# An earlier TensorE warm-up, x's first rows loaded in column halves, and two more single w1 loads in a squared-ReLU MLP

## The chip, the cores and the metric

The kernel runs on one core of one Trainium2 chip. The metric is device time in microseconds (us), median over the runs of a kernel. One run differs from the next by up to about 1.5 us, so every comparison is made between runs on the same chip, and ratios come with a 95% interval. "In the head" means the first 10 us of the kernel.

## The reference

```python
# B, S, D, F = 1, 2048, 576, 4608; all bf16
def reference(x, w1, b1, w2, b2):
    h = jnp.einsum("bsd,df->bsf", x, w1) + b1
    r = jnp.where(h > 0, h, 0)
    return jnp.einsum("bsf,fd->bsd", r * r, w2) + b2
```

## The kernel before

x has four blocks of 512 rows; a block has four row tiles of 128. D = 576 is four chunks of 128 columns and a rest of 64. The kernel keeps w1 in SBUF as pairs of 64-row halves (`w1h`) and runs 36 by 9 by 4 such half-height products at full width, then the second product. All of that is dense. The part that matters here is the head: before the steady matmuls can start, the first 512 rows of x have to be loaded and transposed on TensorE, and the first four column tiles of h are computed from a plainly loaded piece of w1 (`qn`, chunks 0 to 3 of 128 by 512, "quads") so that the big w1 load has time to arrive.

```python
load_x(nc.sync, 0)          # 144 KB each: 128 rows of x, all 576 columns
load_x(nc.scalar, 1)
load_quad(nc.sync, 0)       # 128 KB each: w1 rows c*128.., columns 0..511
load_quad(nc.scalar, 1)
load_quad(nc.sync, 2)
load_x(nc.scalar, 2)
load_x(nc.sync, 3)
load_quad(nc.scalar, 3)
nc.scalar.activation(out=warm[:], ..., func=ACT.Relu)   # brings the activation table
for h in range(2):
    load_rest(nc.sync, h)                               # w1's last 64 rows, 64 KB in all
for j0, n in ((2, 1), (3, 1), (4, 1), (5, 1), (6, 2), (8, 2), (10, 2), (12, 2), (14, 4)):
    for h in range(2):
        load_w1(nc.sync, h, j0, n, slice(0, NH))        # pairs of w1, n at a time
# issue_at_barrier: loads that wait for nothing are moved ahead of the opening barrier's wait
...
for i in range(NWARM):      # 5 warm-up matmuls, 128x512, on constants
    nc.tensor.matmul(wps[:], lhsT=ones[:, 0:P], rhs=ones[:], ...)
...
transpose_chunks(0, (0,), (V,))        # half 0 = row tiles 0 and 1; chunk 0, copied out by VectorE
transpose_chunks(0, (1,), (A,))
fill(HALF)                             # one more matmul on constants, 128x256
full_mm(0, 0)                          # half 0, chunk 0: four matmuls 128x256
transpose_chunks(0, (2, NC), (A, V))
full_mm(0, 1)
transpose_chunks(0, (3,), (A,))
full_mm(0, 2)
transpose_chunks(1, (0, 1), (V, A))    # needs row tiles 2 and 3
full_mm(0, 3)                          # needs w1 chunk 3
transpose_chunks(1, (2, NC), (A, V))
full_mm(1, 0)
...                                    # half 1, the rest, then the steady a_step(0, 2), a_step(0, 3) ...
```

## Time and profile before

| | before |
|---|---|
| median of the first three runs | 290.34 us (289.94 to 290.49) |
| span in the profile | 289.1 us |
| TensorE busy | 285.0 us (99%) |
| first warm-up, first transpose, first real matmul | 0.78, 2.87, 3.67 us |
| first steady matmul (w1h) | 9.90 us |
| release of TensorE's full clock, by the clock record | 6.29 us |

The clock record is the trace's own list of the stretches in which TensorE's clock was granted in full; "release" is the start of the first one. In the views, PE is TensorE's matmuls, PEld its weight loads, DVE VectorE, ACT ScalarE, POOL GpSimd and SP SyncE; a q behind the name marks what the engine's instruction queue issues, such as a load.

From the page of before, the busy times and the chain of work that ended last:

```profile
span 289.1 us, 4821 instructions
...
PE 285.0 (99%) x2068; PEld 187.6 (65%) x2079; DVE 79.3 (27%) x195; ACT 95.5 (33%) x153; POOL 1.5 (1%) x8
...
PE 99%; issue 0%; DVE 0%
```

So TensorE is the bound, and only its head can be shortened. The timeline of TensorE in before (start us, length us, line, operation, count) shows the head. Two things are to be seen. Nothing idles by more than 0.16 us. And the clock is half at first: the four matmuls of 3.67 us start 0.21 us apart, those of 6.79 us 0.11 us apart. The page's granted-clock row reads full speed throughout; this half clock is seen only in the spacing of the matmuls and in the clock record.

```profile
0.78 2.29 PE L150 MATMUL wps<-const-bfloat16-1.0 128*128 128x512 bf16 x5 [0.78 <-PEq L340]
2.87 0.63 PE L167 MATMUL tp<-ident,w_sb 128*128 128x128 bf16 x4
3.30 0.42 PE L153 MATMUL wps<-const-bfloat16-1.0 128*128 128x256 bf16 x1
3.67 1.01 PE L213 MATMUL ph<-w_sb 128*128 128x256 bf16 x4
...
5.97 0.76 PE L213 MATMUL ph<-w_sb 128*128 128x256 bf16 x4
6.57 0.39 PE L167 MATMUL tp<-ident,w_sb 128*128 128x128 bf16 x4
6.79 0.60 PE L213 MATMUL ph<-w_sb 128*128 128x256 bf16 x4
...
9.90 1.46 PE L198 MATMUL ph<-w_sb,w1h 64*128 64x512 bf16 x12
```

The weight loads of before show one wait for w1 later, at pair 6 (in brackets: idle time before the group, and what ended it):

```profile
17.76 1.30 PEld L198 LDWEIGHTS <-w1h 64*128 64x128 bf16 x14 [0.21 <-DMA w1h<-in_w_dram]
```

### The profile page before, as it was taken

The numbers are of one execution on the slowest core, as the hardware profiler recorded it, in microseconds if no ns is written. First come the engines' busy times: TensorE is split into PE (matmuls) and PEld (weight loads), VectorE is DVE, ScalarE is ACT, GpSimd is POOL, SyncE is SP. The second block draws the span as 40 slices with busy tenths as digits, with TensorE's granted clock in tenths as the row PEclk, the third lists the DMA queues.
The fourth block names the chain that finished last, engine by engine and source line by source line (L and its number), as shares of the span: only waits on it lengthen the run. The fifth ranks groups of instructions, "written<-read, shape, count | busy, mean of one in ns | idle before, by whom it ended". The sixth has DMA issues, their size and how long they took to land.

```text
span 289.1 us, 4821 instructions
## 1 busy us (share of the span) xinstructions
PE 285.0 (99%) x2068; PEld 187.6 (65%) x2079; DVE 79.3 (27%) x195; ACT 95.5 (33%) x153; POOL 1.5 (1%) x8
## 2 busy tenths in 40 slices
PE   8999999999999999999999999999999999999996
PEld 5568888888888888888855444444444444444454
DVE  1644454444445444444420011111100111111111
ACT  3666666666666666666620000000000000000000
POOL 2000000000000000000000000000000000000000
PEclk9999999999999999999999999999999999999999
DMA  7999998900300006100000100000000000000000
GB/s 206 217 216 197 178 198 178 328 14 2 114 11 0 3 2 196 51 0 2 0 2 19 20 20 20 20 23 0 20 20 23 20 20 20 23 22 20 20 23 20
DMA packets 34229, 18.01 MB, mean 62 GB/s; under 512 B 19348, under 2 KB 34208, under 8 KB 34208
## 3 DMA queue, kind: packets, MB, share of 16 engines
q1 hardware_dynamic: 33600, 17.14, 25.0%
q10 hardware_dynamic: 576, 0.56, 0.6%
q8 instruction: 16, 0.26, 0.4%
q14 instruction: 5, 0.04, 0.0%
q0 software_dynamic: 32, 0.01, 0.0%
HBM read 11.94 MB, written 2.36 MB: 49 GB/s over the span
## 4 chain that ended last, share of the span: by engine, by line
PE 99%; issue 0%; DVE 0%
PE ph L198 47%; PE po L316 43%; PE pc L302 5%; PE ph L213 2%; PE wps L150 1%; PE tp L167 1%; PE ph L239 0%; DVE o_sb L318 0%; PE wps L153 0%; PE b1T_ps L232 0%
## 5 line engine op out<-in xcount | busy, mean ns | idle before, releaser
L198 PEld LDWEIGHTS <-w1h 64*128 64x128 bf16 x1260 | 115.0, 94 | 21.1 <-DMA w1h<-in_w_dram 0.2
L182 ACT ACTIVATE r<-ph,b1T 128x512 bf16<-128x512 f32 x144 | 90.8, 684 | 48.5 <-PE ph L198 46.6
L198 PE MATMUL ph<-w_sb,w1h 64*128 64x512 bf16 x936 | 101.3, 376 | 0.0
L316 PE MATMUL po<-w_sb,hT 128*128 128x512 bf16 x423 | 92.9, 379 | 0.5
L316 PEld LDWEIGHTS <-hT 128*128 128x128 bf16 x432 | 42.2, 98 | 51.1 <-issue 0.4
L184 DVE TENSOR_TENSOR hT<-r 128x512 bf16<-128x512 bf16 x108 | 45.9, 425 | 54.7 <-ACT r L182 54.7
L318 DVE TENSOR_TENSOR o_sb<-po,b_bc 128x512 bf16<-128x512 f32 (+2 forms) x17 | 11.2, 660 | 116.7 <-PE po L316 109.7
L198 PE MATMUL ph<-xT,w1h 64*128 64x512 bf16 x324 | 35.2, 376 | 0.0
L316 PE MATMUL po<-w_sb,w1h 128*128 128x512 bf16 (+2 forms) x178 | 31.2, 336 | 0.1
L316 PEld LDWEIGHTS <-w1h 128*128 128x128 bf16 x180 | 16.2, 98 | 15.3
L184 DVE TENSOR_TENSOR w1h<-r 128x512 bf16<-128x512 bf16 x36 | 15.3, 425 | 19.7 <-ACT r L182 19.7
L302 PE MATMUL pc<-hT,w_sb 128*64 128x512 bf16 x108 | 15.7, 379 | 0.0
L302 PEld LDWEIGHTS <-w_sb 128*64 128x64 bf16 x144 | 8.1, 110 | 7.6 <-issue 0.4
L302 PE MATMUL pc<-w1h,w_sb 128*64 128x512 bf16 x36 | 7.9, 379 | 0.0
L304 ACT ACTIVATE oc<-pc,b2T 128x512 bf16<-128x512 f32 x2 | 1.4, 687 | 13.8 <-PE pc L302 13.8
L213 PE MATMUL ph<-w_sb 128*128 128x256 bf16 x32 | 5.5, 314 | 0.0
L312 DVE COPY o_sb<-oc 128x64 bf16<-128x64 bf16 x16 | 2.7, 172 | 9.4 <-DMA oc<-oc 9.4
L213 PEld LDWEIGHTS <-w_sb 128*128 128x128 bf16 x32 | 3.3, 112 | 0.7 <-DMA w_sb<-in_w_dram 0.2
L160 DVE COPY w_sb<-tp 128x256 bf16<-128x256 bf16 x5 | 1.5, 291 | 6.5 <-PE tp L167 6.5
L150 PE MATMUL wps<-const-bfloat16-1.0 128*128 128x512 bf16 x5 | 2.3, 622 | 0.8 <-PEq L340 0.8
L167 PE MATMUL tp<-ident,w_sb 128*128 128x128 bf16 x20 | 2.7, 265 | 0.0
L167 PEld LDWEIGHTS <-w_sb 128*128 128x128 bf16 x20 | 2.1, 122 | 0.9 <-DMA w_sb<-in_x_dram 0.6
(28 smaller groups left out, 11.3 us busy)
## 6 DMA issues: line engine op xcount, KB each, us to landing
w_sb<-in_w_dram SPq DMA_DIRECT2D x6, 864.0 KB, 7.4
w1h<-in_w_dram SPq DMA_DIRECT2D x10, 288.0 KB, 7.8
out_dram<-o_sb SPq DMA_DIRECT2D x15, 144.0 KB, 1.7
w1h<-in_w_dram SPq DMA_DIRECT2D x8, 144.0 KB, 3.6
w1h<-in_w_dram SPq DMA_DIRECT2D x2, 576.0 KB, 9.5
w_sb<-in_x_dram SPq DMA_DIRECT2D x2, 144.0 KB, 3.0
w_sb<-in_x_dram ACTq DMA_DIRECT2D x2, 144.0 KB, 3.1
w_sb<-in_w_dram SPq DMA_DIRECT2D x2, 128.0 KB, 3.3
```

The source lines that it names most:

```text
L150: nc.tensor.matmul(wps[:], lhsT=ones[:, 0:P], rhs=ones[:], start=(i == 0), stop=(i == NWARM - 1))
L160: nc.vector.tensor_copy(out=dst, in_=src)
L167: nc.tensor.transpose(tp[:, i * P:(i + 1) * P], xs[:, 2 * half + i, d0:d0 + P], ident[:])
L182: nc.scalar.activation(out=r[:], in_=bk[:], func=ACT.Relu, bias=b1T[:, ft:ft + 1], scale=1.0)
L184: nc.vector.tensor_tensor(out=hT_of(b, ft), in0=r3, in1=r3, op=ALU.mult)
L198: nc.tensor.matmul(bk[h][:], lhsT=w1h[rows, c, j * P:(j + 1) * P], rhs=xT[b][rows, place(h, c), :], start=(i == 0), stop=(i == NH - 1))
L213: nc.tensor.matmul(bk0[q][:, cols], lhsT=qn[:, c, q * P:(q + 1) * P], rhs=xT[0][:, c, cols], start=(half == 0 and c == 0), stop=False, ski ...
L302: nc.tensor.matmul(pc[h * H:(h + 1) * H, :], lhsT=w2(ft, DM, D), rhs=hT_of(2 * pr + h, ft), start=(ft == 0), stop=(ft == NFT - 1))
L304: nc.scalar.activation(out=oc[:, pr, :], in_=pc[:], func=ACT.Identity, bias=b2T[:], scale=1.0)
L312: nc.vector.tensor_copy(out=o_sb[:, DM:D], in_=o_tr[pr][:, jj, h * H:(h + 1) * H])
L316: nc.tensor.matmul(po[:, 0:e - a], lhsT=hT_of(b, ft)[:, jj, :], rhs=w2(ft, a, e), start=(ft == 0), stop=(ft == NFT - 1))
L318: nc.vector.tensor_tensor(out=o_sb[:, a:e], in0=po[:, 0:e - a], in1=b2_bc[:, a:e], op=ALU.add)
```

## The change

The intent: begin the warm-up 0.4 us sooner by placing it ahead of the opening barrier's wait (with its own constant, written by VectorE), bring the first transposes' data sooner by loading only 256 columns of row tiles 0 and 1 first and the other 320 behind w1's chunks 0 and 1, and avoid the wait at pair 6 by loading pairs 6 and 7 singly. The order of the head's work follows the new arrival order. Ten loads in place of eight do not all fit ahead of the barrier: each of the first eight has a completion semaphore of its own, later ones wait for an earlier one to be done. So row tile 3 and chunk 3 are now issued after the barrier.

```diff
-    load_x(nc.sync, 0)
-    load_x(nc.scalar, 1)
+    first, later = slice(0, 2 * P), slice(2 * P, D)
+    load_x(nc.sync, 0, first)
+    load_x(nc.scalar, 1, first)
     load_quad(nc.sync, 0)
     load_quad(nc.scalar, 1)
+    load_x(nc.sync, 0, later)
+    load_x(nc.scalar, 1, later)
     load_quad(nc.sync, 2)
     load_x(nc.scalar, 2)
     load_x(nc.sync, 3)
+    nc.scalar.activation(out=warm[:], ..., func=ACT.Relu)
     load_quad(nc.scalar, 3)
-    nc.scalar.activation(out=warm[:], ..., func=ACT.Relu)
...
-    for j0, n in ((2, 1), (3, 1), (4, 1), (5, 1), (6, 2), (8, 2), ...):
+    for j0, n in ((2, 1), (3, 1), (4, 1), (5, 1), (6, 1), (7, 1), (8, 2), ...):
...
+    one = const.tile([P, 1], BF16, name="one")
+    nc.vector.memset(one[:], 1.0)
+    def warm_at_barrier(nc):   # moves this memset and the 5 warm-up matmuls
+        ...                    # ahead of each engine's wait at the opening barrier
+    nc.at_finalize(warm_at_barrier)
...
-    ones = nc.const_aps.tensor(1.0, [P, SB], BF16)
+    ones = one[:].to_broadcast([P, SB])
...
     transpose_chunks(0, (1,), (A,))
-    fill(HALF)
     full_mm(0, 0)
-    transpose_chunks(0, (2, NC), (A, V))
     full_mm(0, 1)
-    transpose_chunks(0, (3,), (A,))
+    transpose_chunks(0, (2,), (V,))
+    transpose_chunks(0, (3, NC), (A, V))
     full_mm(0, 2)
```

Left out here: w2's chunks 4 and 5, and 2 and 3, each become one load, and b2's last 64 values are loaded by GpSimd. All that happens after 8 us, far ahead of its use.

## The prediction

> **What bounds it.** The page gives a 289.1 us span, TensorE busy 285.0 (99%); the chain of waits is 99% PE. Only the head can be shortened: the timeline has the first w1h matmul (L198) at 9.90 us, and from there PE shows no idle to 60 us (groups view, 0.0 before L198).
>
> In the head (PE timeline): first warm-up 0.78 us, five at 0.427 us apiece; first transpose 2.87; one filler; first real matmul 3.67. 256-column matmuls start 0.213 us apart until about 6.3, then 0.109: the clock doubles 5.5 us after PE's first matmul. The Trainium skill ("TensorE: Matmul & The Clock Gate", Part 1) says the clock is released after a busy, free-running window of about 3.4 us, so the moment varies from run to run. This trace shows the doubling; the variation no trace here shows yet. By that estimate release falls 3.4 to 6.8 us after the start, and one microsecond of it is worth 0.5 us.
>
> **What changes, costed.**
> 1. The warm-up moves ahead of the barrier's wait. PE arrives at the barrier at 0.32 us and is let go at 0.68; its weight load could follow at about 0.39, after VectorE's one-column memset. Gain in start 0.39 us. With an unmoved clock release this is worth half, 0.2 us; if release moves too, 0.39.
> 2. The filler (0.21 us) goes, but it filled a wait for the chunk-0 copy (transpose to copy to matmul, 0.37 us in all): worth 0.
> 3. x's first halves carry 128 KB in place of 288 KB ahead of w1's chunks 0 and 1, which landed at 3.45 and 3.93. At about 270 KB/us (landings between 2.6 and 5.6 us) they land 0.5 us earlier; needed, since PE asks 0.4 us earlier.
> 4. w1's chunk 3 is issued by ScalarE after its table load (1.28 us, ending 3.43) and a wait for an earlier landing: about 3.5 us, not 1.58, so it lands near 6.2 (was 5.56). PE wants it about then. ScalarE's copy of chunk 1 stands behind that issue: about 4.0, not 3.55. Cost 0 to 0.4 us.
> 5. w1 pairs 6 and 7 singly: before, pair 6 landed at 17.72 and PE's weight load had to wait for it (17.76, 0.2 us), so an earlier head would have been lost there. Single halves landed every 0.75 us, so pair 6 now lands near 14.5 and pair 7 near 15.7. Pair 8 (before 20.31, wanted 21.6) slips to about 20.8 and becomes the next floor, some 0.5 us below the old one.
> 6. Merged w2 loads and b2's tail on GpSimd: off the chain (loads at 47 us and later; w2 is wanted after 169): 0.
>
> Bytes and matmuls after 10 us are unchanged, hence 279 us as before. Expected: L198 starts at about 9.4, span about 288.6, a gain of 0.4 to 0.5 us.
>
> **Prediction.** 289.9 us, 8 in 10 between 289.2 and 290.5. Faster by over 2%: 0.01; within 2%: 0.98; slower by over 2%: 0.01.
>
> **What would show it.** Right: first warm-up at 0.35 to 0.45 us; first transpose near 2.5; first real matmul near 3.3; L198 near 9.4; no weight load waiting for w1h at pair 6. Wrong: the warm-up still at 0.7 or later; PE waiting before chunk 1 (ScalarE's copy) or chunk 3 (its landing) for more than 0.4 us; a wait for w1h at pair 8.
>
> **What would make it wrong.** The release of the clock is the widest term: a window more or less is up to 1.7 us either way, larger than the change. New pauses early in the head could make a window count as idle and put release 3.4 us later. Chunk 3 landing late, or pair 8 after 21 us, would give the gain back.

## The result, and the profile after

The changed kernel took 290.74 us (median of 6 runs, 290.55 to 291.05) against 290.41 us (6 runs, 289.94 to 291.31). A ratio here and below is the mean of one kernel's fast runs over the mean of the other's of the same rounds, so not quite the ratio of the medians: 1.0009, interval 0.9992 to 1.0026. On another chip, later, the changed kernel again: 290.88 against 290.29, ratio 1.0019 (1.0000 to 1.0038). Within 2% as predicted, but no gain, and outside the predicted range of 289.2 to 290.5.

The page of after:

```profile
span 288.8 us, 4821 instructions
...
PE 284.7 (99%) x2067; PEld 133.6 (46%) x2078; DVE 79.7 (28%) x197; ACT 95.3 (33%) x152; POOL 3.2 (1%) x11
```

TensorE's timeline in after:

```profile
0.38 2.31 PE L172 MATMUL wps<-one 128*128 128x512 bf16 x5 [0.38 <-DVE one L147]
2.49 0.63 PE L185 MATMUL tp<-ident,w_sb 128*128 128x128 bf16 x4
3.29 1.87 PE L231 MATMUL ph<-w_sb 128*128 128x256 bf16 x8 [0.17 <-DVE w_sb L178]
4.95 0.66 PE L185 MATMUL tp<-ident,w_sb 128*128 128x128 bf16 x6
5.75 0.60 PE L231 MATMUL ph<-w_sb 128*128 128x256 bf16 x4
6.18 0.39 PE L185 MATMUL tp<-ident,w_sb 128*128 128x128 bf16 x4
6.59 0.61 PE L231 MATMUL ph<-w_sb 128*128 128x256 bf16 x4
...
9.71 1.46 PE L216 MATMUL ph<-w_sb,w1h 64*128 64x512 bf16 x12
```

The start came as intended: the warm-up at 0.38, the transposes at 2.49, the first real matmul at 3.29 in place of 3.67. The clock record has the release at 5.26 us, which is 1.03 us before that of the other trace, by itself worth about 0.5 us (half of it, as matmuls run twice as fast afterwards). Still the steady part begins only 0.19 us sooner (9.71 against 9.90). From the first real matmul on, the head took 6.42 us where it had taken 6.23 with a later clock.

The start-to-start times have three new pauses: 0.38 us before 3.29, 0.31 before 5.75 and 0.19 before 6.59. The first two end with a copy of a transposed chunk (chunk 0 and chunk 2), though w1's chunks 0 and 2 landed only 0.1 us before these two ended (3.20 and 5.65). The third is plain in the weight loads of after, which name the loads waited for:

```profile
3.24 1.43 PEld L231 LDWEIGHTS <-w_sb 128*128 128x128 bf16 x8 [0.39 <-DMA w_sb<-in_w_dram]
...
5.69 0.37 PEld L231 LDWEIGHTS <-w_sb 128*128 128x128 bf16 x4 [0.27 <-DMA w_sb<-in_w_dram]
...
6.59 0.33 PEld L231 LDWEIGHTS <-w_sb 128*128 128x128 bf16 x4 [0.19 <-DMA w_sb<-in_w_dram]
```

By the completion records in the two traces (the moment when the last of a load's 16 parts had landed):

| load | before, us | after, us |
|---|---|---|
| x row tiles 0, 1 (after: first 256 columns) | 2.21, 2.62 | 2.04, 2.22 |
| w1 chunks 0, 1 | 3.45, 3.93 | 3.20, 3.63 |
| x's other 320 columns, tiles 0, 1 | with the above | 4.12, 4.32 |
| w1 chunk 2 | 4.70 | 5.65 |
| x row tiles 2, 3 | 4.88, 5.30 | 5.87, 6.11 |
| w1 chunk 3 | 5.56 | 6.54 |

The first four loads came 0.2 to 0.4 us sooner. The last four came about 1 us later, though no byte was added. Chunk 3's first matmul starts 0.05 us after chunk 3 has landed, and the steady part 3.12 us after that. Pair 6 of w1 was complete at 16.38 us in place of 17.72, 1.1 us before its use (9.71 plus four steps of 1.94 us), and no weight load waited for w1h. Chunk 3's load was issued at 3.22 us, while ScalarE's table load was still running:

```profile
2.15 1.28 ACT L118 ACT_TABLE_LOAD   x1 [2.15 <-ACTq L357]
3.22 0.34 ACTq L95 DMA_DIRECT2D w_sb<-in_w_dram  x1
3.45 0.20 ACT L118 ACTIVATE warm<-const-float32-1.0 128x1 f32<-128x1 f32 x1
3.60 0.37 ACT L176 COPY w_sb<-tp 128x256 bf16<-128x256 bf16 x1
```

### The profile page after: what moved, and what is told of

It reads as the page before. It is cut to its first block, busy times and chain, and to the rows that moved or that the text cites. A ratio compares the mean times of both kernels' runs of the same rounds, so it can differ in the third digit from the quotient of the medians.

```text
span 288.8 us, 4821 instructions
## 1 busy us (share of the span) xinstructions
PE 284.7 (99%) x2067; PEld 133.6 (46%) x2078; DVE 79.7 (28%) x197; ACT 95.3 (33%) x152; POOL 3.2 (1%) x11
## 4 chain that ended last, share of the span: by engine, by line
PE 98%; issue 0%; DVE 0%; DVEq 0%
PE ph L216 47%; PE po L333 43%; PE pc L319 5%; PE ph L231 2%; PE wps L172 1%; PE tp L185 0%; DVE w_sb L178 0%; PE ph L256 0%; DVE o_sb L335 0%; DVE one L147 0%; PE b1T_ps L249 0%; DVEq L357 0%
## 5 line engine op out<-in xcount | busy, mean ns | idle before, releaser
L216 PEld LDWEIGHTS <-w1h 64*128 64x128 bf16 x1260 | 61.3, 94 | 74.6
L231 PEld LDWEIGHTS <-w_sb 128*128 128x128 bf16 x32 | 3.2, 108 | 1.4 <-DMA w_sb<-in_w_dram 0.8
L172 PE MATMUL wps<-one 128*128 128x512 bf16 x5 | 2.3, 628 | 0.4 <-DVE one L147 0.4
L176 ACT COPY w_sb<-tp 128x256 bf16<-128x256 bf16 x4 | 1.5, 372 | 2.7 <-PE tp L185 2.7
```

The costliest lines, as they stand in the source:

```text
L172: nc.tensor.matmul(wps[:], lhsT=ones[:, 0:P], rhs=ones[:], start=(i == 0), stop=(i == NWARM - 1))
L176: nc.scalar.copy(out=dst, in_=src)
L216: nc.tensor.matmul(bk[h][:], lhsT=w1h[rows, c, j * P:(j + 1) * P], rhs=xT[b][rows, place(h, c), :], start=(i == 0), stop=(i == NH - 1))
L231: nc.tensor.matmul(bk0[q][:, cols], lhsT=qn[:, c, q * P:(q + 1) * P], rhs=xT[0][:, c, cols], start=(half == 0 and c == 0), stop=False, ski ...
```

## The experiments

Three or four kernels went to one chip, each kernel with one profiled and five timed rounds against before (six runs in all; e6 and e17 have five). Means are given beside medians, because differences are small. The theories named in the expectations:

- A: the split of x makes the head's last loads late, and TensorE is tied to them. A2: it is the split itself, not the two late issues.
- B: luck of the clock's release alone. B2: release follows the start of steady work.
- C: the new order exposes two copies. D: both cost. E: two floors, delivery and clock. G, N: the early start costs by itself, or that is noise.

| run | what | median us | mean, and minus before's mean | ratio (interval) | release us | chunk 3 landed | steady start |
|---|---|---|---|---|---|---|---|
| changed kernel, first | all of it | 290.74 | 290.77, +0.25 | 1.0009 (0.9992 to 1.0026) | 5.26 | 6.54 | 9.71 |
| e1_warm_only | early warm-up | 290.58 | 290.53, +0.01 | 0.9999 (0.9985 to 1.0014) | 5.75 | 6.07 | 9.62 |
| e2_x_whole | changed, x loads of before | 290.56 | 290.61, +0.09 | 1.0002 (0.9987 to 1.0017) | about 4.4 | 6.24 | 9.41 |
| e3_split_only | x loads of the change | 290.92 | 290.94, +0.42 | 1.0013 (0.9999 to 1.0028) | 4.40 | 6.21 | 9.38 |
| e4_w1_only | pairs 6, 7 singly | 290.35 | 290.47, -0.05 | 1.0000 (0.9982 to 1.0017) | 4.49 | 5.82 | 9.05 |
| e6_after_old_order | changed, order of before | 290.82 | 290.83, +0.61 | 1.0022 (1.0010 to 1.0034) | about 4.6 | 6.81 | 9.98 |
| e8_eight_loads_old_order | x split, eight loads | 291.04 | 291.38, +1.16 | 1.0041 (1.0021 to 1.0060) | 8.52 | 6.29 | 11.34 |
| e9_eight_loads_new_order | same, new order | 290.87 | 291.14, +0.92 | 1.0032 (1.0007 to 1.0057) | 4.15 | 6.56 | 10.07 |
| e10_one_warmup | before, 1 warm-up | 290.75 | 290.91, +0.70 | 1.0028 (1.0015 to 1.0040) | 5.75 | 6.41 | 9.58 |
| a2_changed_again | all of it | 290.88 | 290.87, +0.54 | 1.0019 (1.0000 to 1.0038) | 8.46 | 7.02 | 11.13 |
| e12_changed_no_chunk3 | changed, 128 KB fewer | 290.19 | 290.50, +0.18 | 1.0007 (0.9985 to 1.0028) | 4.69 | none | 9.25 |
| e13_before_no_chunk3 | before, 128 KB fewer | 290.23 | 290.16, -0.17 | 0.9995 (0.9981 to 1.0008) | 4.63 | none | 9.29 |
| e11_whole_x_rest_later | early, w1, rest later | 291.19 | 291.00, +0.67 | 1.0030 (1.0017 to 1.0044) | 4.56 | 5.50 | 8.98 |
| e14_six_warmups_at_barrier | early, six warm-ups | 290.47 | 290.45, +0.35 | 1.0010 (0.9997 to 1.0023) | 4.88 | 6.64 | 9.81 |
| e5_warm_and_w1 | early, w1 | 290.78 | 291.02, +0.92 | 1.0034 (1.0011 to 1.0056) | 5.17 | 6.13 | 9.37 |
| e16_warm_and_rest_later | early, rest later | 290.52 | 290.63, +0.53 | 1.0016 (1.0002 to 1.0030) | 5.00 | 6.50 | 9.67 |
| b2_before_as_control | before itself | 290.13 | 290.19, -0.23 | 0.9992 (0.9979 to 1.0004) | about 3.6 | 5.93 | 9.10 |
| e1b_warm_only_again | early warm-up | 290.66 | 290.63, +0.21 | 1.0007 (0.9994 to 1.0019) | 5.72 | 5.92 | 9.57 |
| e17_warm_only_no_chunk3 | early, 128 KB fewer | 290.04 | 290.07, -0.35 | 0.9988 (0.9975 to 1.0001) | about 4.0 | none | 8.90 |

The three right-hand columns are of the one traced execution of each, the release by the clock record or, where "about", by the spacing of the matmuls. The timed runs have no trace. The control sets the scale: before against itself was off by 0.23 us, so a single difference of that size proves nothing.

### Taking the change apart

**Early warm-up alone** (`warm_at_barrier` and the new constant put into before):

> The kernel before with one part of the change: the warm-up ahead of the barrier's wait. Theory A (late delivery: the split of x moves the last head loads from 5.56 to 6.54 us and TensorE is tied to them): here loads keep their old times, so w1's chunk 3 lands near 5.6, no TensorE pause above 0.25 us in the head, and the first w1h matmul comes 0.2 to 0.4 us earlier than before's for the same clock release. Mean 290.1 to 290.3 against about 290.5 for before, unless pair 6 (landing near 17.7) holds it up: then a pause there and the gain is gone. Theory B (luck of the clock's release alone): same as before within noise, release anywhere from 3.4 to 6.8 us after the first warm-up.

```diff
+    nc.vector.memset(one[:], 1.0)
+    nc.at_finalize(warm_at_barrier)
-    ones = nc.const_aps.tensor(1.0, [P, SB], BF16)
+    ones = one[:].to_broadcast([P, SB])
```

Its mean was that of before. The interval reaches 0.4 us each way, so this run alone does not exclude the gain expected; the trace shows where it went. TensorE stands waiting for x behind its warm-up, which it did not do before. The weight loads of the transposes:

```profile
2.57 0.10 PEld L186 LDWEIGHTS <-w_sb 128*128 128x128 bf16 x1 [0.78 <-DMA w_sb<-in_x_dram]
2.95 0.23 PEld L186 LDWEIGHTS <-w_sb 128*128 128x128 bf16 x3 [0.28 <-DMA w_sb<-in_x_dram]
```

The first real matmul starts at 3.62 us against 3.67. The 0.4 us at the front became idle time behind the warm-up: in before the warm-up ended at 2.87 us, 0.25 us after x's second row tile had landed. The steady part came 0.28 us sooner (9.62 against 9.90), and the 0.54 us by which the release was earlier accounts for 0.27 of that. So the 0.2 to 0.4 us expected at the same release did not come, and chunk 3 landed at 6.07 us, not near 5.6.

**The changed kernel with x whole** (the eight loads of before put back):

> The changed kernel with its x loads put back (x whole, eight loads at the barrier, w1 chunk 3 among them); all else as changed. Theory A: chunk 3 lands near 5.6 in place of 6.54, the pause before its matmuls (0.19 us) goes, and the first w1h matmul comes at 9.0 to 9.5 us against 9.71; mean 290.1 to 290.4 against 290.8 for the changed kernel. Theory C (the order without the filler exposes two copies, 0.37 and 0.31 us): no better than the changed kernel, 290.6 to 290.9, with both pauses still there.

```diff
-    load_x(nc.sync, 0, first)     # and the other halves; chunk 3 behind the table load
+    load_x(nc.sync, 0)            # the eight loads as before
```

Chunk 3 landed at 6.24 us, not 5.6, and its matmul began 0.05 us later, at 6.29. Copies cost a pause of 0.32 us before chunk 2's matmuls. The mean, 290.61, is at the lower edge of theory C's band and 0.09 us above before, so it decides little by itself.

**The split loads alone** (the x loads of the change put into before):

> The kernel before with only the x loads of the change (halves, chunk 3 issued after the table load). Theory A: loads land as late as in the changed kernel (chunk 3 near 6.5, x rows 2 and 3 near 5.9 and 6.1), TensorE pauses before chunk 3, first w1h matmul not before 9.7 us; time 290.6 to 291.0 and a narrow spread. Theory B: as before, mean 290.5.

```diff
-    load_x(nc.sync, 0)            # eight loads
+    load_x(nc.sync, 0, first)     # ten loads, in the changed kernel's order
```

The time came out as theory A has it: 0.42 us above before, the interval just reaching 1. The trace missed A's figures: chunk 3 landed at 6.21, not near 6.5, and the steady part did not wait until 9.7. Chunk 3's matmul started at 6.26. With a release as early as 4.40 us the steady part began at 9.38 us all the same, and then stood at pair 6:

```profile
17.72 1.19 PEld L201 LDWEIGHTS <-w1h 64*128 64x128 bf16 x14 [0.69 <-DMA w1h<-in_w_dram]
```

TensorE lost 0.36 us there. So the part of the change that loads pairs 6 and 7 singly does take away a real wait, but one that appears only when the head is early and pair 6 late (17.68 us here). It also means that e3's 0.42 us cannot all be put down to the head: in its trace 0.36 us was lost at pair 6, which the changed kernel does not wait for.

**Pairs 6 and 7 singly, alone** (one line: `(6, 2)` becomes `(6, 1), (7, 1)`):

> The kernel before with only w1 pairs 6 and 7 loaded singly. If pair 6's landing (17.72 us, weight load waiting 0.2 us) limited before's runs, those with an early clock release gain: mean 290.0 to 290.3, lowest below 289.7. If it did not limit: mean 290.5, as before. In the trace pair 6 should land near 14.5 to 15.5 and no weight load wait for w1h.

The mean was that of before (-0.05 us); the lowest run was not below 289.7. Pair 6 was complete at 14.58 us, and no load waited. No sign, then, that pair 6 limits before's ordinary runs, within noise of 0.23 us.

**The changed kernel with the order and filler of before:**

> The changed kernel with only the head's order of transposes and first matmuls put back, filler included. So far, with H the first w1h matmul less half the moment of the clock's release (which takes the clock's luck out): before 6.76, warm-up alone 6.75, w1 alone 6.81, but split alone 7.18, whole x in the new order 7.19, changed kernel 7.08. Theory D (two separate costs: the split's late loads, the new order's exposed copies): here the 0.31 us pause before chunk 2's matmuls goes, but the loads' lateness stays: waits for x's later halves (about 4.2 us) and for chunk 3 (near 6.5). H 6.85 to 7.05; mean 290.5 to 290.7. Theory A (lateness alone sets it): H stays 7.05 to 7.2, since chunk 3 holds the head whatever comes first. Theory C (order alone): H 6.4 to 6.6.

```diff
     transpose_chunks(0, (1,), (A,))
+    fill(HALF)
     full_mm(0, 0)
+    transpose_chunks(0, (2, NC), (A, V))
     full_mm(0, 1)
-    transpose_chunks(0, (2,), (V,))
-    transpose_chunks(0, (3, NC), (A, V))
+    transpose_chunks(0, (3,), (A,))
```

Worse than expected: 0.61 us above before, the interval clear of 1. In its trace all three chunks were waited for:

```profile
3.42 0.55 PEld L235 LDWEIGHTS <-w_sb 128*128 128x128 bf16 x4 [0.46 <-DMA w_sb<-in_w_dram]
...
5.75 0.33 PEld L235 LDWEIGHTS <-w_sb 128*128 128x128 bf16 x4 [0.54 <-DMA w_sb<-in_w_dram]
...
6.85 0.33 PEld L235 LDWEIGHTS <-w_sb 128*128 128x128 bf16 x4 [0.44 <-DMA w_sb<-in_w_dram]
```

Putting the old order back saved nothing, so theory C falls as the main cause. Theory D's correction for the clock falls too: with an early release the head does not follow the clock at all. It starts its steady part at 9.98 us, 3.12 us after chunk 3's matmul, whatever the clock did.

### Is it the late issue, or the split itself?

These two kernels split x and yet have only eight loads, all issued by 2.1 us, by taking the later columns of both tiles in one load and row tiles 2 and 3 in one:

```diff
+    load_x(nc.sync, slice(0, 2), later)
+    load_x(nc.scalar, slice(2, 4))
     load_quad(nc.sync, 2)
     load_quad(nc.scalar, 3)
```

> A version meant to beat both: warm-up at the barrier, w1 six pairs singly, x's first halves of 256 columns, but the later 320 columns of both row tiles in one load and row tiles 2 and 3 in one load, so that there are again eight loads, all issued at the barrier (w1 chunk 3 by 2.05 us, not 3.2), and the old order of transposes with the filler. Theory D: chunk 3 lands by 6.0, no pause over 0.2 us after the first real matmul at 3.3 us, H 6.4 to 6.55, mean 290.15 to 290.35. If instead smaller packets slow the whole delivery (theory A2: it is the split itself, not the two late issues), chunk 3 lands at 6.3 or later and H stays near 7.0, mean 290.6 or more.

> The same eight loads with the changed kernel's order, no filler. Theory D: the 0.31 us pause for chunk 2's copy is back, so H is 0.2 to 0.3 above that of the old order with the same loads: 6.65 to 6.85, mean 290.3 to 290.55. Theory A: no difference between the two orders.

Both were meant to beat before and both were worse, 1.16 and 0.92 us above. Chunk 3, issued at 1.59 us, landed at 6.29 and 6.56, no sooner than in the changed kernel, which had issued it at 3.22. In e8's trace TensorE waits for chunk 0 and then for x's later columns:

```profile
3.99 0.56 PEld L233 LDWEIGHTS <-w_sb 128*128 128x128 bf16 x4 [1.03 <-DMA w_sb<-in_w_dram]
5.18 0.34 PEld L187 LDWEIGHTS <-w_sb 128*128 128x128 bf16 x4 [0.63 <-DMA w_sb<-in_x_dram]
```

So the late issue is not needed for the lateness. What all kernels with a split share is a slower delivery at the beginning. The windows view over 1.0 to 2.5 us and 1.0 to 5.2 us (last two numbers: DMA share, GB/s) of before:

```profile
1.00:2.50 1.50, 1.50 (x5) 0.50 (x4) 0.00 (x0) 0.35 (x1) 1.10 (x3) 1.00 0.87 261
1.00:5.20 4.20, 4.20 (x20) 2.36 (x19) 0.35 (x2) 1.91 (x4) 1.10 (x3) 1.00 0.92 282
```

and of after:

```profile
1.00:2.50 1.50, 1.50 (x5) 0.44 (x4) 0.00 (x0) 0.35 (x1) 1.11 (x3) 1.00 0.81 208
1.00:5.20 4.20, 4.03 (x19) 2.26 (x18) 0.29 (x1) 1.81 (x3) 1.11 (x3) 1.00 0.88 251
```

Over 1.0 to 2.5 us the other traces with x whole moved 234 (the control) to 269 GB/s (e11), with one exception, 217 in e17; those with the split moved 194 (a2) to 221 (e6), e3 with its late warm-up 210. Over 1.0 to 5.2 us, in the kernels that load chunk 3, it is 271 to 297 GB/s whole, and 249 to 263 with the split in ten loads; the two with merged loads catch up (273 and 278), but by then TensorE has stood for w1's chunk 0 and x's later columns. The packet records agree: 544 KB of the program's loads had been moved after 3.0 to 3.2 us in every kernel with x whole, and after 3.4 to 3.5 us in every kernel with the split. Chunk 3 landed at 6.57 us on average in the six traces with the split (6.21 to 7.02) and at 6.07 in the eleven with x whole (5.50 to 6.64): half a microsecond apart, but the ranges overlap. Two things go with it, and no run here separates them. Packets were 512 and 640 B in place of 1,152 B. And the first issue held its queue for 0.39 us with 64 KB (after) as with 144 KB (before), so the first pair of issues carried 128 KB instead of 288. The Trainium skill ("DMA: Bandwidth & Descriptors", Specifications) puts the smallest transfer for full rate at 512 B; loads whose packets were at and just above that size went with the lower rate.

### How many warm-ups

> The kernel before with one warm-up matmul in place of five: TensorE then idles from about 1.2 us until the first x row lands near 2.2 to 2.6. If the clock's release follows the start of steady work (theory B2), release comes 1.5 to 2 us later on average (6 us or later here) and the mean is 0.5 to 1 us above before: 291.0 to 291.5. If the release does not care about when work begins, the time is that of before, 290.5, and starting the warm-up 0.4 us earlier could not have moved the release either.

With `NWARM = 1` in before the mean rose by 0.70 us, within the 0.5 to 1 us expected of theory B2. The release in the trace came at 5.75 us, a little earlier than it said; and chunk 3 landed at 6.41 with its matmul at 6.47, so in that execution delivery set the steady start, not the clock. The warm-up of before is worth having.

### Two floors

In after, e2, e3, e6 and e10 chunk 3's matmul started 0.05 to 0.06 us after chunk 3's landing; in before, e1 and e4 it came later, at the clock's pace. Theory E: the steady part begins at the later of the two, and chunk 3's landing plus 3.17 us is one of them.

> The changed kernel again, beside before on the same chip. Theory E (two floors): the first w1h matmul starts at the later of what the clock's release allows and w1 chunk 3's landing plus 3.17 us (0.05 to the matmul, 3.12 from it at full clock); with x split, chunk 3 landed at 6.54, 6.21, 6.81, 6.29 and 6.56, with x whole at 5.56, 6.07, 6.24, 5.82 and 6.41. So here chunk 3 lands at 6.2 to 6.8, the first w1h matmul is never before 9.4, and the mean is 0.2 to 0.6 us above before's. Rival (noise): within 0.15 us of before.

The second look at the changed kernel gave 0.54 us above before, as expected; chunk 3's landing lay outside the expected range, at 7.02. Its traced execution was the slowest (292.0 us) and shows something else: release only at 8.46 us. Its timeline:

```profile
2.49 0.63 PE L185 MATMUL tp<-ident,w_sb 128*128 128x128 bf16 x4
3.87 1.89 PE L231 MATMUL ph<-w_sb 128*128 128x256 bf16 x8 [0.75 <-DMA w_sb<-in_w_dram]
...
7.59 1.03 PE L231 MATMUL ph<-w_sb 128*128 128x256 bf16 x4
8.45 0.40 PE L185 MATMUL tp<-ident,w_sb 128*128 128x128 bf16 x4
...
11.13 1.24 PE L216 MATMUL ph<-w_sb,w1h 64*128 64x512 bf16 x9
```

Chunk 0 landed at 3.83 us, so TensorE stood from about 2.91 to 3.87. Chunk 3's issue waits for chunk 0's completion and went out at 3.85, landing at 7.02. The release at 8.46 is 8.1 us after the first matmul, as in e8; in all other traces it is 2.8 to 5.5. The Trainium skill ("TensorE: Matmul & The Clock Gate", Part 1) describes a free-running window of about 3.4 us that has to be busy. The clock records agree with the length: the full clock lasts 283.31 us in 14 of the 16 traces that have such a record and 286.72 us in the other two (e3 and e9), which is 83 and 84 times 3.413. Taken with that length, the window that ended 3.41 us before this release ran from 1.64 to 5.05 us and had 0.96 us, 28%, of idleness. In e8, released at 8.52, the same reckoning gives 1.15 us (34%): 0.87 in one pause and the start of another. Windows that did release, in the other 14 of those traces, had 0.16 us (before) to 0.60 us (e5) of idleness, 5 to 18%. That is an estimate that combines the page's window with these traces; by it, a pause of about 1 us in the early head costs a whole window. Runs as long as these two, 291.9 us and more, of which only these two were traced, were 1 of 12 in the changed kernel, 2 of 6 in e8, 1 of 6 in each of e9, e12 and e5, and none of the 61 of before (289.49 to 291.31).

The next two take the load of chunk 3 away; its matmuls use chunk 2's weights, so the result is wrong (relative error 0.043):

```diff
-    load_quad(nc.scalar, 3)
-    ... lhsT=qn[:, c, q * P:(q + 1) * P], rhs=xT[0][:, c, cols] ...
+    ... lhsT=qn[:, min(c, 2), q * P:(q + 1) * P], rhs=xT[0][:, c, cols] ...
```

> The changed kernel without the load of w1 chunk 3; its matmuls take chunk 2's weights, so the result is wrong on purpose and 128 KB fewer are moved in the head. Theory E: the floor goes, the head is then held by x row tiles 2 and 3 (about 6.0, and 3.39 us of work behind) or by the clock; the first w1h matmul at 9.1 to 9.5 us, mean 0.2 to 0.45 us below the changed kernel of the same call. Rival (pauses for copies and the clock alone set the head): no difference beyond 0.1 us.

> The kernel before without the load of w1 chunk 3, wrong result on purpose in the same way. Theory E: before was mostly held by the clock and only in part by chunk 3 (floor about 9.2 against a clock-bound start of 8.9 to 10.5), so it gains less than the changed kernel does: 0 to 0.2 us below before. If it gains as much as the changed kernel (0.3 or more), the head of both was held by delivery and the split is not what set them apart.

On the same chip the changed kernel's median fell from 290.88 to 290.19 (means 290.87 and 290.50; one of the six runs, 292.08, is as slow as those that miss a window). Before's fell by 0.17 us in the mean. With 128 KB fewer the two kernels are equal by their medians (290.19 and 290.23). In the trace of the changed kernel without chunk 3 those matmuls follow the transposes with no pause:

```profile
5.92 0.39 PE L184 MATMUL tp<-ident,w_sb 128*128 128x128 bf16 x4
6.14 0.60 PE L230 MATMUL ph<-w_sb 128*128 128x256 bf16 x4
```

Theory E came out as expected here, though each of the two differences alone is of the order of the noise.

### Looking for a version that beats both

> Meant to beat both: before with the warm-up at the barrier and w1 six pairs singly, x whole, old order, and the 64 KB of w1's last rows (wanted only at 9.2 us) moved behind pair 2's loads, so chunk 3 has less ahead of it. Theory E: chunk 3 lands at 5.4 to 6.1; first w1h matmul at 9.0 to 9.8 depending on the release; mean 0 to 0.25 us below before. The warm-up's 0.4 us is not gained, as the first transposes wait for x (2.5 to 2.9 us). Not above before by more than 0.1.

```diff
+    nc.at_finalize(warm_at_barrier)
-    for h in range(2):
-        load_rest(nc.sync, h)
...
-    for j0, n in ((2, 1), ..., (6, 2), (8, 2), ...):
+    for j0, n in ((2, 1), ..., (6, 1), (7, 1), (8, 2), ...):
         for h in range(2):
             load_w1(nc.sync, h, j0, n, slice(0, NH))
+        if j0 == 2:
+            for h in range(2):
+                load_rest(nc.sync, h)
```

It did not: 0.67 us above before. Its traced execution was the only fast one (290.04 us, steady start at 8.98, no wait for w1h); the five timed ones were 290.87 to 291.37. To see which part was at fault, and whether an early start without a pause is worth something:

> Before with the warm-up at the barrier and six matmuls in place of five, so that it ends near 2.9 us, when x has landed, as it did before, and no pause opens between warm-up and transposes. x whole, old order, w1 as before. If release follows the start of work (theory B2), it comes 0.4 us earlier on average than in before and the mean is 0.1 to 0.3 us below before's, no run above 291.2. If the early start cannot be turned into time at all (the head is held by delivery as much as by the clock), within 0.1 of before. Real matmuls start at 3.6 to 3.8, not earlier than in before.

> Before with the warm-up at the barrier (five) and w1 six pairs singly; x whole, old order. Each part alone was neutral, so expected within 0.15 us of before. If it is 0.4 or more above, the loss of the last version (291.0 mean) came from these two together, not from moving w1's last rows.

> Before with the warm-up at the barrier and w1's last rows moved behind pair 2's loads. If those rows' place cost the last version its 0.67 us, this one is 0.4 us or more above before too; in the trace the last rows land after 7.2 us and every later w1 pair 0.2 to 0.3 us later, so with pair 6 in one load a wait at pair 6 is likely. Otherwise within 0.15 of before.

Their edits are the early warm-up with, in turn, one more line:

```diff
-    NWARM = 5
+    NWARM = 6                                     # e14
...
+    ... (6, 1), (7, 1) ...                        # e5
...
+        if j0 == 2: load_rest(nc.sync, 0), (.., 1)   # e16, as above
```

All three were above before, by 0.35, 0.92 and 0.53 us, e5 with one run of 292.62. For e14 neither expectation held (0.1 to 0.3 below, or within 0.1). e5 and e16 each met the sign that was to put the fault on its own line, so neither line can be singled out; what the three share is the early warm-up. In e14 and e16 chunk 3 landed late, at 6.64 and 6.50, and its matmul followed at 6.69 and 6.55. Hence: before unchanged, the early warm-up unchanged, and the early warm-up with the two lines that leave out chunk 3:

> The kernel before, unchanged, entered as a kernel under test: a control for the noise, and a second trace of it. Ratio 1.000, its interval holding 1. 1088 KB of the head's bytes moved by 4.8 to 5.1 us. If it differs from its own twin by more than 0.15 us in the mean, differences of that size in the other runs prove nothing.

> Warm-up at the barrier alone, a second time, on whatever chip this falls. The first time it was equal to before (0.9999), while three other versions with the early warm-up and x whole were 0.35 to 0.9 us above. Theory G (the early start itself costs, by a pause behind the warm-up and later loads): 0.2 to 0.5 us above before here. Theory N (noise and the other edits): within 0.15 us.

> Warm-up at the barrier alone, without the load of w1 chunk 3 (wrong result on purpose). Before without that load was 0.17 us below before. If what the early start costs lies in delivery, it goes with the bytes: within 0.15 us of that, that is 0 to 0.3 below before. If it lies in the clock's release or in the pauses before the first matmuls, it stays: 0.1 to 0.4 above before.

The early warm-up alone was 0.21 us above this time, while the control was 0.23 us below, more than its expectation allowed. So whether the early warm-up by itself costs something is left open: six versions with it and x whole lie 0.01 to 0.92 us above before, none below; an interval of the plain one, taken twice, holds 1 both times. None of them shows a gain. Without chunk 3 it was 0.35 us below before, in five runs within 0.24 us of each other, and 0.56 us below its twin with chunk 3 (290.07 against 290.63). This difference is well clear of the control's 0.23: with the early warm-up, 128 KB less to deliver is worth time. In the changed kernel itself the same removal (a2 and e12, 0.36 us in the mean) is not clear of noise.

The control's own trace is the best single view of the two floors. In it the clock was released at about 3.6 us, 2.7 us earlier than in the first trace of the same kernel:

```profile
3.67 0.60 PE L213 MATMUL ph<-w_sb 128*128 128x256 bf16 x4
...
5.55 0.53 PE L167 MATMUL tp<-ident,w_sb 128*128 128x128 bf16 x4
5.97 0.61 PE L213 MATMUL ph<-w_sb 128*128 128x256 bf16 x4
...
9.10 1.24 PE L198 MATMUL ph<-w_sb,w1h 64*128 64x512 bf16 x10
```

All real matmuls run at full clock from the first (3.67), 2.7 us of earlier release should be worth about 1.3 us, and the steady part came 0.80 us sooner. Chunk 3 landed at 5.93; its matmul starts at 5.97; the steady part 3.12 us later. Of the 17 traces with chunk 3's load, eight have its matmul start 0.04 to 0.06 us after its landing: after, e2, e3, e6, e10, e14, e16 and this one.

## Why the prediction was wrong

1. **"The warm-up moves ahead of the barrier's wait ... worth half, 0.2 us; if release moves too, 0.39."** The move was right to 0.01 us (first matmul at 0.38, first real one at 3.29). Its worth was wrong. With x whole it was turned into waiting behind the warm-up (e1). With x split it reached the first real matmul and was spent on later waits.
2. **"The filler goes ... worth 0."** Not separated by itself; the pause it filled was 0.38 us in after. Nothing contradicts it.
3. **"At about 270 KB/us they land 0.5 us earlier" (chunks 0 and 1).** They landed 0.25 and 0.30 us earlier. I took the rate of whole tiles for the split ones; over the first stretch it was 208 GB/s in place of 261. And I carried that gain forward, as if only the order of arrival changed, not the rate. Behind these two the gain turned into a loss: chunk 2 landed 0.95 us later than before, chunk 3 0.98 us.
4. **"Lands near 6.2 ... PE wants it about then ... Cost 0 to 0.4 us."** The mechanism was right, the size was off. Chunk 3 landed at 6.54 and 7.02; its issue was tied to chunk 0's landing (3.22), not to the end of the table load. I named this as a cost beside others. In the traced execution it was the floor: 6.54 and 3.17 make the 9.71 us at which the steady part began, and 6.2 and 3.17 would have made the 9.4 that I expected. Seven other traces stand on the same floor; in e9 it was chunk 2 (landed at 6.25, its matmul at 6.29), in a2 and e8 the clock. I had also read before's landing (5.56) off one trace; in ten other traces that load x whole it landed at 5.50 to 6.64. Before can stand on this floor too, as the control's trace shows.
5. **Order.** I did not count the 0.31 us pause before chunk 2's matmuls that the new order opens. Undoing the order did not help (e6), so it is not what decided.
6. **"The release of the clock is the widest term", and "new pauses early in the head could make a window count as idle".** The traces bear out both: release came at 3.6 to 6.3 us in most traces, and at 8.5 in two where pauses of about 1 us had opened. I held this as a risk; it is a part of the changed kernel's mean (1 run of 12).
7. **"Pair 6 now lands near 14.5 ... Pair 8 ... slips to about 20.8."** They landed at 16.38 and 21.31, later than I reckoned from the pace of the single loads. The wait at pair 6 is gone all the same, but it mattered only in heads that are early (e3), and the change does not make the head early.
8. **w2 and b2: 0.** The steady part and the end took 279.1 us in after and 279.2 in before, as predicted.
9. **"Span about 288.6, a gain of 0.4 to 0.5 us", and from it 289.9 us.** This step failed on its own, and cost about half of the miss. The gain was reckoned from a trace whose execution took 290.84 us, with a release as late as 6.29, but it was taken off the median, 290.34. In every run the time is 1.7 to 1.8 us more than the span, so a span of 288.6 means about 290.35 us: what before's median run took already. Put the other way, and as an estimate from these numbers, before's median (290.41, less 1.75 and 279.2) has its steady part at about 9.5 us. A start at 9.4 was a gain over the traced execution alone.

Taken together: 289.9 missed 290.74 by 0.84 us. About 0.45 of that is step 9, a gain over a late execution booked against the median. The rest is steps 3 and 4: the sum treated delivery as a small correction, and in the traced execution chunk 3's landing, 0.34 us later than reckoned, put the steady part at 9.71 in place of 9.4. That delivery holds the timed runs too is inferred: they have no trace, and only the early warm-up with and without chunk 3 (e1b and e17) differ by more than the noise.

## What to carry to other kernels

Before starting the compute of a head sooner, ask when the last byte it needs lands: in the eight traces here that stood on that floor, the head ended at that landing plus the fixed work behind it, and an earlier warm-up only moved idle time from in front of it to behind it. Take the time from which a gain is subtracted from the same execution as the trace, or trace several: one trace of before here was 0.5 us slower than its median. Splitting a load to get its first part sooner has to be priced by what it does to the last part, and with several traces, since here the landing of one and the same load lay anywhere from 5.5 to 6.6 us in kernels that load x the same way. Look for pauses of a microsecond in the early head: in the two traces that had one, the full clock came a window later. Fitting the warm-up's length to the arrival of the data was tried once (e14) and showed no gain, 0.35 us above before.

## What the Trainium skill lacked or had wrong

- "TensorE: Matmul & The Clock Gate", Part 1, gives release after a busy window of about 3.4 us or more. The control's release came between 3.5 and 3.7 us, at most 2.9 us after TensorE's first matmul (0.78), so a window need not be busy throughout. The page does not say how much idleness it may have; here 0.60 us passed (e5) and 0.96 us did not (a2), as far as the estimate above goes. With one warm-up (e10) the release at 5.75 fits as well: counted back, its window begins at 2.33, behind the 1.29 us of idleness after that warm-up, and has 0.59 us of its own.
- The same page, Part 4, says that the full clock does not engage for transposes. In before the transposes' starts are 0.107 us apart before the release and 0.056 us after it, half, as for the matmuls of 256 columns.
- "DMA: Bandwidth & Descriptors", Specifications, gives 512 B as enough for full rate. With first packets of 512 B and then 640 B the head moved 194 to 221 GB/s over 1.0 to 2.5 us, against 234 to 269 with 1,152 B (217 in e17); packet size and load size were not separated.
- "DMA: Bandwidth & Descriptors", Why a DMA increments its semaphore by 16 and not by 1, tells that a load's 16 parts finish independently, but not by how much: w1's chunk 2 in after landed from 3.91 to 5.65 us.
- "ScalarE: Activation LUTs", What ACT_TABLE_LOAD costs, has 1,283 ns, which the trace shows exactly (1.283 us). It does not say that a DMA issue standing behind it in ScalarE's program goes out while it runs (3.22 us, the load ending at 3.43).
- The profile's granted-clock row reads 1.00 while matmuls run at half pace in the head; the clock record begins only with the release (6.29 us in before), and 4 of the 20 traces have none. No page says so of this row.
